# Adding the output projection's head-pair sums in DRAM in the first half of an attention kernel

## The chip, the cores and the metric

The kernel runs on one core of a Trainium2 chip. A core has five engines with a queue of their own each: TensorE (PE in the profile, its weight loads shown apart as PEld), VectorE (DVE), ScalarE (ACT), GpSimd (POOL) and SyncE (SP), which here only issues DMAs. Each engine works through its queue in order, and an instruction that waits for a semaphore holds up all that stands behind it on the same engine. Sixteen DMA engines move the data that any queue asks for. The metric is the device time of one execution in microseconds.

## The reference

With x of shape 2048 x 640, the reference computes a gated attention block in float32:

```python
xn = layernorm(x)
q  = (xn @ wq), as 32 heads of 128
p  = softmax(q @ k.T / sqrt(128))     # over the last 512 cached keys of each head
s  = concat_heads(p @ v) @ wo         # 4096 -> 640
g  = silu(relu(xn @ w1 + b1)**2 @ w2 + b2)
out = x + s * g
```

What matters here is the projection with `wo`: it sums over all 32 heads. The kernel takes the heads in pairs, so each 640 x 512 tile of `s` is a sum of 16 terms.

## The kernel before

The 2048 rows are cut into four tiles of 512. First the gate `g` is computed for three of the tiles; then comes the attention, in two halves (`hf`) of two tiles (`t`) each. Within a half the order is: for each of 16 head pairs (`g`), for each of the two tiles, for each of the two heads: one unit. There are 128 units, numbered `i`; an odd `i` ends a head pair for its tile. The gate of the fourth tile is worked into the start and the end of the attention.

Every product is made of three matmuls on a high and a low part of each operand. So a high part is made by ScalarE (a copy that rounds) and a low part by VectorE or GpSimd (a subtraction). One unit on the engines:

- TensorE: 12 matmuls for the scores `s` (`s_mm`, four banks), 15 for the query projection of a later unit (`q_mm`), 12 for the output `o` of the unit before (`v_mm`, four chunks of keys, the first two of which use the first half of the probabilities), and on average 15 for the projection with `wo` (`r_mm`; 30 for each head pair, in five blocks `d` of 128 output columns).
- VectorE: column maxima (`max_fold`), the shift `e = s - max` (`shift`), low parts of `q` and `o`, the sums of the softmax (`s_fold`), the normalisation (`o_norm`), and the additions of `r_acc`.
- ScalarE: `expo` (exponentials, two halves `k`), `p_hi` (high parts of the probabilities), `gather`, `q_hi`, `o_hi`, and the high parts of the weights (`prep`).
- GpSimd: `p_lo(i, 0)`, `s_add`, `p_lo(i, 1)` (low parts of the two halves of the probabilities, and the sum for the softmax), and the low parts of the weights (`prep`).
- SP: it writes the maxima to DRAM (`m_d`) and loads them back spread over all partitions (`bm`), the same for the softmax sums (`s_d` from `rows`, back as `bs`), and loads the raw weights behind `bs`.

The order of all this is written out by hand: `at(when, f, ...)` and `on(when, f, ...)` put a call into a plan with a nominal time, the plan is sorted by time, and the calls are issued in that order (`PERIOD` is the nominal unit). So each engine's queue holds its instructions in the order of the plan. The wrapper `Ordered` at lines 69 to 85 issues them, which is why nearly all of them carry line 77 in the profile and are told apart by the names of their tiles.

The projection's results come in two PSUM banks that are shared with the queries (`bank`, line 566). `r_acc` (line 753) empties them:

```python
        if g == 0:
            ...
            act.activation(ACC[hf, t][:, d, :], pr, AF.Copy)
        else:
            a = ACC[hf, t][:, d, :]
            dve.tensor_tensor(a, pr, a, op=ALU.add)
```

So for the first head pair ScalarE copies the bank to an accumulator in SBUF, and for the other 15 VectorE adds the bank to it. The tag `acc` has two buffers of 128 x 5 x 512, one for each tile of a half. The five `r_acc` of a head pair lie at about 3.0, 3.3, 4.0, 4.3 and 4.7 units after the start of its last unit in the order `d0`, `d1`, `d3`, `d2`, `d4` (line 1098; nominal times in `R_AT`, line 1038): `d0` and `d1` in an even unit, `d3`, `d2` and `d4` in an odd one. At the end of the first half `store_acc` (line 766) writes the accumulators to the DRAM tensor `s_d[t]`, and much later, one by one among the units of the second half, `load_finish`, `finish_gate` and `finish` read them back and make the output. In the second half the accumulator stays in SBUF to the end.

Of the kernel before, what the change touches and what calls it, by code (L numbers as in the profile page):

```python
# [8 lines left out]
F32 = mybir.dt.float32  # L9
F32R = mybir.dt.float32r  # L10
AF = mybir.ActivationFunctionType
ALU = mybir.AluOpType
AX = mybir.AxisListType

P = 128
NT = 512
# [9 lines left out]
def kernel(  # L26
# [20 lines left out]
    DC = D // P  # L47
# [21 lines left out]
    class Ordered:  # L69
# [13 lines left out]
    pe, dve, act, pool, sp = (  # L83
        Ordered(e) for e in (nc.tensor, nc.vector, nc.scalar, nc.gpsimd, nc.sync)
    )
# [5 lines left out]
    s_d = [dpool.tile([P, DC, NT], F32, name=f"s_d{t}") for t in range(NTILE // 2)]  # L91
# [15 lines left out]
    keep = ctx.enter_context(tc.tile_pool(name="keep", bufs=1))  # L107
# [375 lines left out]
    def mlp_step(n):  # L483
# [54 lines left out]
    TPH = NTILE // HALF  # L538
# [10 lines left out]
    PERIOD = 12.4  # L549
# [5 lines left out]
    XT, ACC, KT, VV, WQ, WO, Q, E, SC, MB, RD, PT, PO, OT, RB, QPS, FX, CL, PRS, RAW = (  # L555
        {} for _ in range(20)
    )
# [195 lines left out]
    def r_acc(i, d):  # L753
        hf, g, t, h = units[i]
        pr = PRS.pop((i, d))
        if g == 0:
            if d == 0:
                ACC[hf, t] = keep.tile(
                    [P, DC, NT], F32, tag="acc", name=f"acc{hf}_{t}", bufs=TPH
                )  # L760
            act.activation(ACC[hf, t][:, d, :], pr, AF.Copy)
        else:
            a = ACC[hf, t][:, d, :]
            dve.tensor_tensor(a, pr, a, op=ALU.add)

    def store_acc(t, d):
        sp.dma_start(s_d[t][:, d, :], ACC[0, t][:, d, :])

    def load_finish(n, hf, t, d):
        t0 = (hf * TPH + t) * NT  # L770
# [231 lines left out]
    def at(when, f, *a):  # L1002
        plan.append((max(when, 0.0), len(plan), f, a))

    for n in range(HALF * NG):
        hf, g = divmod(n, NG)
# [43 lines left out]
    for i in range(NU):  # L1050
        t0 = i * PERIOD

        def on(when, f, *a):
            at(t0 + when, f, *a)

        hf, g, t, h = units[i]
        for c in range(KC):
            on(0.68 * c, align, i, SLOTS[c])
            on(0.68 * c, s_mm, i, c)
        on(0.68 * KC - 0.6, align, i, SLOTS[KC])  # L1060
        qs = [(i + AHEAD, 3.45 if i % G and i > UPG else 4.3, 4.1)]
        if i == 0:
            qs = [(1, 2.8, 4.1), (2, 9.1, PERIOD - 5.2)]
        elif i < UPG:
            qs = [(i + 2, 4.9 if i == 3 else 4.2, 4.1)]
        for n, q_at, low in qs if i + AHEAD < NU else ():
            for c in range(DC):
                on(q_at + 0.68 * c, q_mm, n, (c,))
            on(q_at + 3.5, q_hi, n)
            on(q_at + low, q_lo, n)  # L1070
        for c in range(KC):
            on(0.8 + 0.68 * c, max_fold, i, c)
        on(3.95, gather, i, "m")
        on(4.1, row, i, "m")
        for c in range(KC):
            on(10.4 + 0.4 * c, shift, i, c)
        on(11.7, expo, i, 0)
        on(12.7, p_hi, i, 0)
        on(13.8, expo, i, 1)
        on(PERIOD + 4.0, p_hi, i, 1)  # L1080
        on(13.9, p_lo, i, 0)
        on(16.2, s_add, i)
        on(PERIOD + 6.2, s_fold, i)
        on(PERIOD + 8.0, gather, i, "s")
        on(PERIOD + 8.5, row, i, "s")
        on(18.6, p_lo, i, 1)
        for c in range(KC):
            on(PERIOD + 8.5 + 0.68 * c, v_mm, i, c)
        on(2 * PERIOD + 4.2, o_norm, i)
        on(2 * PERIOD + 4.9, o_hi, i)  # L1090
        on(2 * PERIOD + 5.5, o_lo, i)
        if i % G == G - 1:
            for d in range(DC):
                last = i == NU - G - 1
                if i < NU - 1:
                    for when, js in (R_AT_END if last else R_AT)[d]:
                        on(when, r_mm, i, d, js, (R_BANK_END if last else R_BANK)[d])
                    on(when + 0.68 * len(js), r_acc, i, d)
                if g == NG - 1 and hf == 0:
                    at((i + (3, 4, 5, 4, 5)[d] + (t and d in (0, 3, 4))) * PERIOD + 4.3, store_acc, t, d)  # L1100
                    w = (NU // 2 + 9 + 4 * (t * DC + d)) * PERIOD
                    for k, n in enumerate("sxg"):
                        at(w + k * PERIOD - 0.6, load_finish, n, 0, t, d)
                    at(w + 3 * PERIOD - 0.7, finish_gate, 0, t, d)
                    at(w + 3 * PERIOD - 0.7, finish, 0, t, d)
# [10 lines left out]
    for item in order:  # L1116
        kind, n = item[0], int(item[1:] or 0)
        if kind == "u":
            UP_AT[n] = now
        elif kind == "d":  # L1120
            DOWN_AT[n] = now
            at(now, late_down, n, range(DC))
        elif kind == "r":
            at(now, r_mm, NU - 1, n, range(G), (n + 1) % 2)
            at(now + 1.36, r_acc, NU - 1, n)
        else:
            for k, d in enumerate(range(DC)):
                for f in range(FA, FC):
                    DOWN_AT.setdefault(f, now)
                    at(now + 0.68 * ((FC - FA) * k + f - FA), late_down, f, (d,))  # L1130
                at(now + 0.68 * (FC - FA) * (k + 1), late_gate, d)
        now += STEP[kind]
# [110 lines left out]
```

## Time and profile before

| | |
|---|---|
| median of 3 runs | 1958.72 us (1958.57 to 1959.38) |
| profiled execution, span from first to last instruction | 1956.9 us |
| what lies around the span, against the median | 1.8 us |
| TensorE, weight loads | 1949.2, 1612.5 us busy |
| VectorE, ScalarE, GpSimd | 1537.3, 1187.6, 1376.7 us busy |
| granted TensorE clock | 1.000 |
| DMA on SP's queue (q1) and GpSimd's (q0) | 202.75 MB and 14.42 MB |

No time of its own is given for the profiled execution beside its span; the difference of 1.8 us to the median stands for what lies around. How to read the rows: a row of the timeline gives start, duration, engine, line, operation, the tile written and the tiles read, and in brackets the idle time before and what ended it. A group row gives busy time and mean nanoseconds of one instruction. A row of DMA issues gives the KB of each and the microseconds from issue to landing.

### The profile page before, as it was taken

The page shows a single profiled execution, that of the slowest core. Times are in us where ns is not written, and L with a number is a line of the kernel's source. Part 1 is how long each engine was busy: PE and PEld are TensorE (multiplying, and loading weights), DVE is VectorE, ACT ScalarE, POOL GpSimd, SP SyncE. Part 2 cuts the span into 40 slices and gives each one's busy share as a digit, 9 for nine tenths or more (in the row PEclk, how much of TensorE's full clock was granted, in tenths as well). Part 3 has the DMA queues.
Part 4 walks back from the last instruction along what each step waited for, and adds up shares of the span by engine and source line. Part 5 has one row for each costly group of instructions (what it writes and reads, how often), then busy time and mean ns, then how long its engine had stood idle before and what let it go on. Part 6 is the DMA issues. An engine that isn't in the chain of part 4 may idle for free.

```text
span 1956.9 us, 28182 instructions
## 1 busy us (share of the span) xinstructions
PE 1949.2 (100%) x8612; PEld 1612.5 (82%) x8612; DVE 1537.3 (79%) x2638; ACT 1187.6 (61%) x2040; POOL 1376.7 (70%) x757
## 2 busy tenths in 40 slices
PE   9999999999999999999999999999999999999998
PEld 7888888888888888888888888888888888888887
DVE  6523337788888888888888878888888888888865
ACT  5432336766666666666666676666666666666643
POOL 2121226888888888888888888888888888888841
PEclk9999999999999999999999999999999999999999
DMA  6330454333333332332335434433333333332353
GB/s 189 88 119 28 185 198 130 97 94 92 93 92 93 92 92 92 92 92 93 93 91 179 141 117 109 114 114 114 114 113 114 113 114 114 98 92 92 85 189 118
DMA packets 127892, 219.13 MB, mean 112 GB/s; under 512 B 23452, under 2 KB 38086, under 8 KB 126470
## 3 DMA queue, kind: packets, MB, share of 16 engines
q1 hardware_dynamic: 124742, 202.75, 34.3%
q0 software_dynamic: 2864, 14.42, 1.8%
q8 instruction: 77, 1.26, 0.2%
q14 instruction: 65, 0.53, 0.1%
q10 hardware_dynamic: 144, 0.16, 0.0%
HBM read 193.41 MB, written 23.87 MB: 111 GB/s over the span
## 4 chain that ended last, share of the span: by engine, by line
PE 99%; DVE 0%; DMA 0%; ACT 0%; issue 0%; POOL 0%; POOLq 0%
PE pq L77 22%; PE r L77 22%; PE o L77 18%; PE s L77 18%; PE ph L431 7%; PE ly L77 2%; PE py L101 2%; PE py L100 2%; PE py L102 2%; PE lu L77 2%; PE eu L77 1%; PE ph L398 0%; PE py L454 0%; PE py L453 0%; DMA xb<-in_x_dram 0%; PE px L77 0%
## 5 line engine op out<-in xcount | busy, mean ns | idle before, releaser
L77 POOL TENSOR_TENSOR pt<-e,pt 128x1024 fp32r<-128x1024 f32 x256 | 615.8, 2405 | 113.6 <-ACT pt L77 68.2
L77 PE MATMUL r<-ot,wo 128*128 128x512 f32 x1920 | 496.6, 389 | 0.0
L77 PE MATMUL pq<-ax,wq 128*128 128x512 f32 x1920 | 456.1, 389 | 0.0
L77 PEld LDWEIGHTS pq<-ax,wq 128*128 128x128 f32 x1920 | 360.4, 188 | 75.2 <-DVE q L77 0.4
L77 PEld LDWEIGHTS r<-ot,wo 128*128 128x128 f32 x1920 | 360.5, 188 | 74.8
L77 PE MATMUL o<-pt,wv 128*128 128x512 f32 x1536 | 369.2, 389 | 0.0
L77 PE MATMUL s<-q,wk 128*128 128x512 f32 x1536 | 369.0, 389 | 0.0
L77 DVE TRANSPOSE_TENSOR_REDUCE rdm<-s 128x16 f32<-128x512 f32 x512 | 347.6, 712 | 6.0 <-PE s L77 5.8
L77 ACT ACTIVATE e<-e 128x1024 f32<-128x1024 f32 x256 | 269.8, 1054 | 123.8 <-DVE e L77 80.5
L77 PEld LDWEIGHTS o<-pt,wv 128*128 128x128 f32 x1536 | 288.3, 188 | 60.1 <-POOL pt L77 0.4
L77 PEld LDWEIGHTS s<-q,wk 128*128 128x128 f32 x1536 | 288.4, 188 | 59.8
L77 DVE TENSOR_TENSOR e<-s,bm 128x512 f32<-128x512 f32 x512 | 312.3, 665 | 5.8 <-DMA bm<-m_d 5.4
L77 POOL TENSOR_TENSOR su<-e,e 128x1024 f32<-128x1024 f32 x128 | 309.2, 2415 | 0.0
L77 ACT ACTIVATE pt<-e 128x1024 fp32r<-128x1024 f32 x256 | 271.9, 1062 | 6.9
L77 DVE TENSOR_TENSOR acc<-r,acc 128x512 f32<-128x512 f32 x300 | 203.6, 679 | 12.7 <-PE r L77 12.4
L77 ACT ACTIVATE rdm<-rdm 32x64 f32<-32x64 f32 x384 | 97.7, 254 | 182.1 <-DVE rdm L77 179.0
L77 DVE TRANSPOSE_TENSOR_REDUCE rds<-su 128x32 f32<-128x1024 f32 x128 | 158.4, 1237 | 0.3 <-POOL su L77 0.3
L77 DVE TENSOR_TENSOR ot<-o,ot 128x512 fp32r<-128x512 f32 x128 | 88.5, 692 | 86.1 <-ACT ot L77 86.1
L77 ACT ACTIVATE q<-pq 128x512 fp32r<-128x512 f32 x128 | 76.7, 599 | 113.6 <-PE pq L77 113.6
L431 PE MATMUL ph<-xT,w1s 128*128 128x512 f32 x585 | 139.0, 389 | 0.0
L431 PEld LDWEIGHTS ph<-xT,w1s 128*128 128x128 f32 x585 | 109.7, 188 | 22.8
L77 ACT ACTIVATE rds<-rds 32x32 f32<-32x32 f32 x384 | 89.7, 234 | 60.1 <-DVE rds L77 56.6
(137 smaller groups left out, 1942.3 us busy)
## 6 DMA issues: line engine op xcount, KB each, us to landing
bm<-m_d SPq DMA_DIRECT2D x128, 256.0 KB, 3.2
bs<-s_d SPq DMA_DIRECT2D x128, 256.0 KB, 4.0
qr<-in_wq_dram SPq DMA_DIRECT2D x64, 320.0 KB, 4.5
or<-in_wo_dram SPq DMA_DIRECT2D x64, 320.0 KB, 4.7
kr<-in_kT_dram SPq DMA_DIRECT2D x64, 256.0 KB, 4.3
vr<-in_v_dram SPq DMA_DIRECT2D x64, 256.0 KB, 4.3
xT_d<-xT POOLq DMA_DIRECT2D x6, 1280.0 KB, 7.6
ax<-xT_d SPq DMA_DIRECT2D x4, 1280.0 KB, 11.3
```

The costliest lines, as they stand in the source:

```text
L77: ins = method(*args, **kwargs)
L100: nc.tensor.matmul(ps, ah, bh, start=first and i == 0, stop=False)
L101: nc.tensor.matmul(ps, ah, bl, start=False, stop=False)
L102: nc.tensor.matmul(ps, al, bh, start=False, stop=last and i == n - 1)
L431: nc.tensor.matmul(ph, w1s[f][i][:, c, :], xs[j][:, c, :], start=k == 0, stop=k == len(order) - 1,)
```

## The change

In the first half (`hf == 0`) `r_acc` lets ScalarE copy every bank, for all 16 head pairs, to a tile of the tag `acc`, which is now taken anew for each head pair. After the copy of the last block (`d == DC - 1`) GpSimd's queue issues one DMA of the whole tile (1280 KB) to `s_d[t]`: a plain write for the first head pair, and for the other 15 a DMA that adds to what is there, in descriptors of at most 5120 bytes, so two for each of the 128 partitions. The ten stores `store_acc` on SP's queue and their places in the plan are gone. The second half is as before.

```diff
     def r_acc(i, d):
         hf, g, t, h = units[i]
         pr = PRS.pop((i, d))
-        if g == 0:
+        if hf == 0:
+            if d == 0:
+                ACC[hf, t] = keep.tile(
+                    [P, DC, NT], F32, tag="acc", name=f"part{i}", bufs=TPH
+                )
+            act.activation(ACC[hf, t][:, d, :], pr, AF.Copy)
+            if d == DC - 1:
+                how = {} if g == 0 else {"accum_op": ALU.add, "max_dma_last_dim": 2 * DC * NT}
+                pool.dma_start(s_d[t], ACC[hf, t], **how)
+        elif g == 0:
             if d == 0:
                 ACC[hf, t] = keep.tile(
                     [P, DC, NT], F32, tag="acc", name=f"acc{hf}_{t}", bufs=TPH
...
         else:
             a = ACC[hf, t][:, d, :]
             dve.tensor_tensor(a, pr, a, op=ALU.add)
-
-    def store_acc(t, d):
-        sp.dma_start(s_d[t][:, d, :], ACC[0, t][:, d, :])
...
                 if g == NG - 1 and hf == 0:
-                    at((i + (3, 4, 5, 4, 5)[d] + (t and d in (0, 3, 4))) * PERIOD + 4.3, store_acc, t, d)
                     w = (NU // 2 + 9 + 4 * (t * DC + d)) * PERIOD
```

## The prediction

> **What bounds the kernel now.** Begin with the page's head, busy shares and chain of waits.
>
> ```profile
> span 1956.9 us, 28182 instructions
> PE 1949.2 (100%) x8612; PEld 1612.5 (82%) x8612; DVE 1537.3 (79%) x2638; ACT 1187.6 (61%) x2040; POOL 1376.7 (70%) x757
> PE 99%; DVE 0%; DMA 0%; ACT 0%; issue 0%; POOL 0%; POOLq 0%
> ```
>
> The chain is TensorE from end to end. Next, the timeline of TensorE gives the start of the score matmuls of two units far apart, and of two neighbours:
>
> ```profile
> 383.03 1.29 PE L77 MATMUL s<-q,wk 128*128 128x512 f32 x5
> 603.35 2.88 PE L77 MATMUL s<-q,wk 128*128 128x512 f32 x12
> 615.59 2.88 PE L77 MATMUL s<-q,wk 128*128 128x512 f32 x12
> 1851.83 1.52 PE L77 MATMUL s<-q,wk 128*128 128x512 f32 x6
> ```
>
> 615.59 - 603.35 = 12.24 us, and (1851.83 - 383.03) / 12.24 = 120.0 units: one pace, in both halves and while the first half's sums are handed over. A unit is 54 matmuls (12 scores, 12 outputs, 15 queries, 15 projection), so 226.7 ns each. No unit is shorter than another, so TensorE waits for nobody here, and freeing VectorE can't shorten a unit. What the change can do to the time is add a wait.
>
> The wait nearest to happening is the one for GpSimd's low part of the probabilities, `p_lo(i, 1)`. It happened once, in the start-up:
>
> ```profile
> 341.22 2.40 POOL L77 TENSOR_TENSOR pt<-e,pt 128x1024 fp32r<-128x1024 f32 x1
> 343.68 0.99 PEld L77 LDWEIGHTS o<-pt,wv 128*128 128x128 f32 x5 [0.37 <-POOL pt L77]
> ```
>
> GpSimd ended at 343.62 and the eighth weight load of `o` started 0.06 us later: that load needs `p_lo(i, 1)`.
>
> **Part 1: 150 sums leave VectorE, 150 copies come to ScalarE.** By groups of instructions:
>
> ```profile
> L77 DVE TENSOR_TENSOR acc<-r,acc 128x512 f32<-128x512 f32 x300 | 203.6, 679 | 12.7 <-PE r L77 12.4
> L77 ACT ACTIVATE acc<-r 128x512 f32<-128x512 f32 x20 | 11.8, 588 | 3.8 <-PE r L77 3.6
> ```
>
> VectorE loses 150 x 0.679 = 101.9 us (half of the 300, the first half's), ScalarE gains 150 x 0.588 = 88.2 us. Neither sets the pace, so the gain is nothing; the question is what stands behind each copy on ScalarE's queue. The trace already holds the answer: the first head pair of the second half is copied by ScalarE in the same places, at full pace. Its timeline, with an even unit starting at 1154.15 (615.59 + 44 x 12.24):
>
> ```profile
> 1148.51 2.43 POOL L77 TENSOR_TENSOR pt<-e,pt 128x1024 fp32r<-128x1024 f32 x1
> 1149.85 2.68 PEld L77 LDWEIGHTS o<-pt,wv 128*128 128x128 f32 x12
> 1151.91 0.58 ACT L77 ACTIVATE acc<-r 128x512 f32<-128x512 f32 x1
> 1152.08 1.57 POOL L77 TENSOR_TENSOR wq<-qr,wq 128x640 fp32r<-128x640 f32 x1 [1.14 <-ACT wq L77]
> 1152.25 2.48 DVE L77 TENSOR_TENSOR e<-s,bm 128x512 f32<-128x512 f32 x4 [0.20 <-DMA bm<-m_d]
> 1156.26 2.41 POOL L77 TENSOR_TENSOR pt<-e,pt 128x1024 fp32r<-128x1024 f32 x1 [1.35 <-issue]
> 1160.99 2.41 POOL L77 TENSOR_TENSOR pt<-e,pt 128x1024 fp32r<-128x1024 f32 x1
> 1162.09 2.68 PEld L77 LDWEIGHTS o<-pt,wv 128*128 128x128 f32 x12
> 1164.05 2.43 DVE L77 TENSOR_TENSOR e<-s,bm 128x512 f32<-128x512 f32 x4
> 1166.59 0.60 ACT L77 ACTIVATE acc<-r 128x512 f32<-128x512 f32 x1 [0.15 <-PE r L77]
> ```
>
> Read off the margins. The eighth weight load is due 7 x 0.2267 = 1.59 us after the first. Odd unit: 1149.85 + 1.59 - 0.06 - (1148.51 + 2.43) = 0.44 us. Even unit: 1162.09 + 1.59 - 0.06 - (1160.99 + 2.41) = 0.22 us. In the odd unit ScalarE also has 0.15 us in which the copy of `d3` waits for its matmul, so the even unit's shift (1164.05, the input of that chain) may come 0.15 + 0.44 = 0.59 us later before TensorE waits. Copies alone: cost 0, between 0 and nothing below, since this pair ran at 12.24. Their cover is these 0.2 to 0.6 us, where the same waits had more room before:
>
> ```profile
> 621.50 2.42 POOL L77 TENSOR_TENSOR pt<-e,pt 128x1024 fp32r<-128x1024 f32 x1
> 623.53 2.68 PEld L77 LDWEIGHTS o<-pt,wv 128*128 128x128 f32 x12
> ```
>
> 623.53 + 1.59 - 0.06 - 623.92 = 1.14 us. If the cover goes, each late microsecond is paid once per pair of units.
>
> **Part 2: the DMA on GpSimd's queue.** 32 DMAs are issued (16 head pairs, 2 tiles), 30 of them accumulating. Each waits on GpSimd for the copy of `d4`; behind it stand low parts of weights and then `p_lo(i, 0)`. What a plain one costs there:
>
> ```profile
> L77 POOL DMA_DIRECT2D xT_d<-xT x16 | 8.9, 556 | 0.0
> xT_d<-xT POOLq DMA_DIRECT2D x6, 1280.0 KB, 7.6
> bm<-m_d SPq DMA_DIRECT2D x128, 256.0 KB, 3.2
> bs<-s_d SPq DMA_DIRECT2D x128, 256.0 KB, 4.0
> s_d<-acc SPq DMA_DIRECT2D x10, 256.0 KB, 3.9
> ```
>
> For tile 0 the copy of `d4` ends at 1152.49 and the low part of `wq` at 1153.65, and the issue goes between that and `wv`; before `p_lo(i, 0)` GpSimd idles 1.35 us, which hides 0.56. For tile 1 the issue stands one odd unit later, where GpSimd waits for ScalarE's `wo`; more room. An accumulating issue has 256 rows of 5 KB where a plain one has 128, and two reads a row: 0.56 to 4 x 0.56 = 2.2 us. I take about 1 us, nearer the row, and hidden: 0. At 2.2 it would cost 2.2 - 1.35 - 0.22 = 0.6 us for each of tile 0's 15.
>
> SP loses the ten stores of the last row; nothing waits for SP's issue there: 0. Their successor, the last accumulating DMA, is issued near 1127, and the reload of the sums starts at 1191.5 (rows below), so nothing waits there either.
>
> ```profile
> L77 SPq DMA_DIRECT2D s_d<-acc x10: 425/430/435, 1088.4 to 1149.1; - x10
> L77 SPq DMA_DIRECT2D fs<-s_d x10: 375/376/433, 1191.5 to 1632.4; - x10
> ```
>
> A tile's buffer is written again by the `d0` copy of its next pair. For tile 0 the `d4` copy above ends at 1152.49; the `d0` copy of tile 1 is at 1154.60, tile 0's next one two units later, about 1179.1: 26.6 us, and a DMA that lands within that delays no copy.
>
> ```profile
> 1154.60 0.58 ACT L77 ACTIVATE acc<-r 128x512 f32<-128x512 f32 x1
> 1175.62 0.57 ACT L77 ACTIVATE acc<-r 128x512 f32<-128x512 f32 x1
> ```
>
> The second row is tile 1's `d4` copy, two units less 0.77 us after that of tile 0 (1151.91).
>
> **Part 3: what the DMA does to the loads beside it.** This is the disputed term. Two views of the DMA queues, each one microsecond long: GpSimd's queue alone (213 to 214), and beside loads from SP (210 to 211); columns are packets, MB, share of 16 engines.
>
> ```profile
> q0 software_dynamic: 54, 0.43, 101.7%
> ...
> q1 hardware_dynamic: 97, 0.22, 55.6%
> q0 software_dynamic: 33, 0.22, 51.7%
> ```
>
> A plain 1.31 MB takes 1.31 / 0.43 = 3.05 us of all engines. Adding in DRAM moves the bytes up to three times (read both, write one): 3.05 to 9.15 us. No run shows it; with the second read on the same engines at least partly in turn I take 2.5 passes, 7.6 us, one row of 5 KB on an engine 7.6 / 16 = 0.48 us. The loads that share the time (`bs` and two weights, 0.85 MB) add 0.85 / 0.43 = 2.0 us, so the DMA is in flight 9.6 us. Issued at 613.2 (tile 1: 1176.19 less 46 units) or 615.1 (tile 0: 1153.65 less 44 units) in the time of the unit of 603.35, with about 1.1 us to the first byte, it ends near 623.9 or 625.8. These loads lie in it:
>
> ```profile
> 614.63 0.32 SPq L77 DMA_DIRECT2D bs<-s_d  x1
> 620.52 0.33 SPq L77 DMA_DIRECT2D m_d<-rowm  x1
> 621.02 0.68 DVE L77 TENSOR_TENSOR o<-o,bs 128x512 f32<-128x512 f32 x1
> 621.89 0.33 SPq L77 DMA_DIRECT2D bm<-m_d  x1
> ```
>
> `bs` lands at 618.6 and is used at 621.0: 2.4 us of room. `bm` lands at 625.09; the shift that needs it would start at 615.59 + (1164.05 - 1154.15) = 625.49: 0.40 of room, and 0.59 from part 1: 0.99 us. In the shared microsecond three packets of SP went by for one of GpSimd's (97 to 33). `bm` has 8 packets of 2 KB on each engine, so it lets 8/3 = 2.7 rows past: 2.7 x 0.48 = 1.28 us; `m_d` waits for one, 0.48. Late: 1.76 - 0.99 = 0.77 us for tile 0. For tile 1 only about half of `bm` is caught: 0.64 + 0.48 - 0.99 = 0.13. `bs` loses 1.28 of its 2.4.
>
> **Sum.** 15 x 0.77 + 15 x 0.13 = 13.5 us, all on TensorE's path; parts 1 and 2 nothing. Against the profiled span 1956.9 + 13.5 = 1970.4; the median of the runs, 1958.72, lies 1.8 us above that span, so 1972. Ends of the unknown: one pass (ends by 621.3, before `bm` moves) gives 0; three passes (0.57 us a row, both tiles caught in full: 1.52 + 0.57 - 0.99 = 1.10 x 30) gives 33 us, 1992.
>
> **Rivals.**
> *Hidden anyway.* The DMA is through before 621 or the loads slip past, and the time is 1958.7 to 1960. For it: the pair copied by ScalarE ran at 12.24; in the shared microsecond SP's queue still moved 0.22 MB, hardly less than `bm` needs. It decides at two passes: then tile 1's DMA ends at 622.4, before `bm` moves. That VectorE's 102 us bring nothing belongs to this case too.
> *The DMA far slower, or its packets taken in turn one for one.* `bm` then lets 8 rows past: 8 x 0.48 + 0.48 - 0.99 = 3.3 us, in 30 places 100 us: 2058. Against it: the 97 to 33 above; for it: those were loads with a full queue. With rows of 1 us at three for one it is 2.7 + 1 - 0.99 = 2.7, 80 us: 2040; above 26.6 us in flight the copies of ScalarE would wait as well.
> [...]
> *GpSimd's issue becomes the bound.* At 2.2 us each, 15 x 0.6 and for tile 1 about half as much: 13 us, 1972, with SP's loads on time.
>
> **How the numbers follow.** Within 0.2% (3.9 us) is about what a measurement can tell from no change. Chances: `bm` late, 1963 to 1998, 0.40; hidden, 0.31; far slower 0.10 and one for one 0.07, 1998 to 2060; GpSimd's issue, 0.07; another wait that I don't see, 0.02; faster, 0.03, since only start-up waits such as the 0.37 us above could go. Slower: 0.66; same: 0.31; faster: 0.03. The forecast is the first case, 1972, its own range 1963 to 1998; the range for 8 in 10 takes in the hidden case and part of the slow one: 1957 to 2025.
>
> **What the profile after would show.** Right: `acc<-r` 150 on VectorE and 170 on ScalarE; 32 issues on GpSimd's queue; q0 up by 42 MB or more; score starts of the first half more than 12.24 us apart, second half unchanged; VectorE's shift of even units idle before it, released by `bm`; weight loads of `o` idle, released by GpSimd's `pt`; landing of `bm` up in the first half's even units. Wrong: first half at 12.24 (hidden); issues of 2 us on GpSimd with `bm` on time (the third rival); landing over 20 us, with ScalarE's copies waiting for a DMA (the second).

## The result and the profile after

The changed kernel takes 2086.46 us, median of 4 runs (2085.6 to 2089.6), where the kernel before took 1959.05 in 4 runs on the same chip (1958.57 to 1959.92). The ratio is 1.0653, with an interval of 1.0641 to 1.0666. The change costs 127 us, 4.2 us for each of its 30 adding DMAs. That the time rises, because small loads come late and TensorE waits, was forecast. The size was not: 1972 was said, and the range ended at 2025. Nor were the places where TensorE waits.

The page of the changed kernel, in the order in which that of before was read: the span, the busy shares, the chain of waits by engine, and GpSimd's DMA queue (packets, MB, share of 16 engines).

```profile
span 2087.8 us, 28249 instructions
PE 2001.3 (96%) x8612; PEld 1636.1 (78%) x8612; DVE 1450.2 (69%) x2488; ACT 1253.8 (60%) x2190; POOL 1410.5 (68%) x789
q0 software_dynamic: 11312, 56.36, 12.1%
PE 68%; DMA 16%; DVE 7%; ACT 4%; issue 2%; POOL 2%; SPq 0%; POOLq 0%; ACTq 0%
```

The span grew by 2087.8 - 1956.9 = 130.9 us. VectorE lost its 150 sums (1537.3 to 1450.2 us busy), and that brought nothing. The chain, TensorE from end to end before, now goes through a DMA for 16% of the span. Where the time went is in the groups of TensorE's matmuls, and in the group of VectorE's shift (busy us, mean ns, idle before and what ended it):

```profile
L77 PE MATMUL r<-ot,wo 128*128 128x512 f32 x1920 | 510.4, 397 | 38.1 <-DVE q L77 38.1
L77 PE MATMUL s<-q,wk 128*128 128x512 f32 x1536 | 399.1, 412 | 37.2 <-DVE e L77 37.1
...
L77 PE MATMUL o<-pt,wv 128*128 128x512 f32 x1536 | 371.6, 390 | 3.4 <-POOL pt L77 3.4
...
L77 DVE TENSOR_TENSOR e<-s,bm 128x512 f32<-128x512 f32 x512 | 313.2, 668 | 66.8 <-DMA bm<-m_d 65.8
```

TensorE waits 38.1 + 37.2 + 3.4 = 78.7 us in the attention, where its list of waits had none of these before, and it is busy 2001.3 - 1949.2 = 52.1 us longer with the same 8612 matmuls. Together that is 130.8 of the 130.9 us. The list of waits (total us, times, longest) says what is behind both:

```profile
DVE o L77 <- DMA bs<-s_d: 76.9, 17, 5.7
DVE e L77 <- DMA bm<-m_d: 65.8, 18, 6.2
PE r L77 <- DVE q L77: 38.1, 15, 3.4
PE s L77 <- DVE e L77: 37.1, 16, 5.3
```

So there are two places, about one visit for each head pair and tile. Some 16 times the scores wait for VectorE's shift `e`, which waits for the maxima (`m_d`, then `bm`). Some 15 times the projection waits for VectorE's `q`, which stands on its queue behind the normalisation of `o`, which waits for the softmax sums (`bs`).

The first place, a DMA of tile 0, in the timeline of the changed kernel (start, duration, engine, operation, in brackets the idle time before):

```profile
707.39 1.19 POOL L77 DMA_DIRECT2D s_d<-part  x1
...
712.99 0.33 SPq L77 DMA_DIRECT2D m_d<-rowm  x1
...
718.83 0.33 SPq L77 DMA_DIRECT2D bm<-m_d  x1
...
722.17 2.48 DVE L77 TENSOR_TENSOR e<-s,bm 128x512 f32<-128x512 f32 x4 [4.14 <-DMA bm<-m_d]
722.91 4.61 PE L77 MATMUL s<-q,wk 128*128 128x512 f32 x12 [2.45 <-DVE e L77]
```

`bm` reads what `m_d` wrote, and its issue is SP's wait for it: 718.83 - 712.99 = 5.84 us, where the kernel before took 621.89 - 620.52 = 1.37. VectorE then idles 4.14 us and TensorE 2.45. And the twelve scores take 4.61 us instead of 2.88. The second place, a DMA of tile 1:

```profile
734.76 1.20 POOL L77 DMA_DIRECT2D s_d<-part  x1 [1.47 <-ACT part L77]
...
736.18 0.32 SPq L77 DMA_DIRECT2D bs<-s_d  x1
...
746.66 0.70 DVE L77 TENSOR_TENSOR o<-o,bs 128x512 f32<-128x512 f32 x1 [4.87 <-DMA bs<-s_d]
...
750.50 2.58 PE L77 MATMUL r<-ot,wo 128*128 128x512 f32 x6 [2.56 <-DVE q L77]
```

Here `bs` is in flight from 736.18 to about 746.6, 10.4 us, where it took 4.0 before. The DMA queues in windows of the changed kernel (714 to 716, then 743 to 744; packets, MB, share of the engines) show SP's packets beside the adding ones:

```profile
q0 software_dynamic: 80, 0.41, 101.6%
...
q0 software_dynamic: 32, 0.16, 81.4%
q1 hardware_dynamic: 30, 0.06, 18.3%
```

In the first window, one and three microseconds after `m_d` was issued, SP's queue moves no packet at all. Its 80 adding rows took all engines for 2 us, so one row takes 2 x 16 / 80 = 0.40 us. Later, at 743, the two queues go one for one, 32 packets to 30 (a packet in these rows is one row). So the share was none to 80 in one window and 30 to 32 in the other, and neither is the 97 to 33 on which the forecast rested. How many rows go by ahead of `m_d` is measured below, and it is no fixed number.

The slow scores are the granted clock. The view by windows of the changed kernel (the number after the five engines' busy times is the clock):

```profile
719.00:722.90 3.90, 1.46 (x7) 0.89 (x5) 0.73 (x2) 0.00 (x0) 1.76 (x2) 1.00 0.28 73
722.91:727.52 4.61, 4.61 (x13) 3.69 (x14) 3.80 (x6) 3.43 (x4) 1.35 (x1) 0.63 0.51 187
727.52:730.00 2.48, 2.48 (x12) 2.03 (x12) 1.03 (x2) 1.68 (x5) 2.48 (x2) 1.00 0.01 3
```

0.63 over 4.61 us is (1 - 0.63) x 4.61 / 0.5 = 3.4 us at half clock, behind the wait of 2.45 us, and full clock again after it. The trace's clock records hold 23 such stretches, 85.3 us in all, and every one follows a wait of TensorE of 1.8 us or more. But not every such wait has one: of the 29 waits of that length in the attention 6 have none. Two waits of the same 2.56 us show the difference (they end at 864.23 and at 1034.13):

```profile
860.15:863.56 3.41, 1.52 (x7) 0.94 (x5) 2.51 (x4) 1.08 (x2) 0.00 (x0) 1.00 0.13 46
863.56:866.97 3.41, 2.57 (x10) 1.83 (x11) 2.99 (x8) 2.23 (x6) 1.89 (x2) 1.00 0.14 47
1030.82:1034.23 3.41, 0.85 (x5) 0.39 (x3) 2.59 (x4) 1.76 (x5) 0.00 (x0) 1.00 0.19 63
1034.23:1037.64 3.41, 3.41 (x8) 2.68 (x9) 3.20 (x7) 2.39 (x5) 2.66 (x2) 0.50 0.09 32
```

All 23 stretches begin a whole number of times 3.413 us apart and last 3.413 us, two of them twice that, so the attention of this trace can be counted in slots of that length. In 21 slots TensorE idled 1.95 us or more, and every one is followed by a slot at half clock. Of the five with 1.79 to 1.90 us three are. Of those with 1.7 us or less one is, with 1.05 us, and it was itself at half clock. The wait at 1034.13 lies in one slot; the one at 864.23 is split into 1.89 and 0.67 us. The mean clock is 0.979 where it was 1.000: up to 0.021 x 2087.8 = 44 of the 52 us by which TensorE was busy longer (85.3 us at half clock lose 42.7).

The second half is as before; two neighbouring units still stand 12.24 us apart:

```profile
1847.92 2.88 PE L77 MATMUL s<-q,wk 128*128 128x512 f32 x12
...
1860.16 2.88 PE L77 MATMUL s<-q,wk 128*128 128x512 f32 x12
```

### The profile page after: what moved, and what is told of

Same layout as the page of the kernel before. It is cut to its first block, busy times and chain, and to the rows that moved or that the text cites. A ratio compares the mean times of both kernels' runs of the same rounds, so it can differ in the third digit from the quotient of the medians.

```text
span 2087.8 us, 28249 instructions
## 1 busy us (share of the span) xinstructions
PE 2001.3 (96%) x8612; PEld 1636.1 (78%) x8612; DVE 1450.2 (69%) x2488; ACT 1253.8 (60%) x2190; POOL 1410.5 (68%) x789
## 4 chain that ended last, share of the span: by engine, by line
PE 68%; DMA 16%; DVE 7%; ACT 4%; issue 2%; POOL 2%; SPq 0%; POOLq 0%; ACTq 0%
PE r L77 15%; PE s L77 13%; PE pq L77 12%; PE o L77 10%; DMA bs<-s_d 6%; PE ph L431 6%; DMA m_d<-rowm 5%; DMA bm<-m_d 3%; DVE rdm L77 2%; PE ly L77 2%; PE py L101 2%; PE py L100 2%; PE py L102 2%; PE lu L77 2%; DVE rds L77 2%
## 5 line engine op out<-in xcount | busy, mean ns | idle before, releaser
L77 PE MATMUL r<-ot,wo 128*128 128x512 f32 x1920 | 510.4, 397 | 38.1 <-DVE q L77 38.1
L77 PEld LDWEIGHTS r<-ot,wo 128*128 128x128 f32 x1920 | 366.1, 191 | 121.5 <-DVE q L77 44.8
L77 PE MATMUL s<-q,wk 128*128 128x512 f32 x1536 | 399.1, 412 | 37.2 <-DVE e L77 37.1
L77 PEld LDWEIGHTS s<-q,wk 128*128 128x128 f32 x1536 | 306.8, 201 | 113.1 <-DVE e L77 46.4
L77 DVE TENSOR_TENSOR e<-s,bm 128x512 f32<-128x512 f32 x512 | 313.2, 668 | 66.8 <-DMA bm<-m_d 65.8
L77 POOL TENSOR_TENSOR wv<-vr,wv 128x512 fp32r<-128x512 f32 x64 | 90.0, 1406 | 108.8 <-ACT wv L77 101.7
L77 DVE TENSOR_TENSOR o<-o,bs 128x512 f32<-128x512 f32 x128 | 87.0, 679 | 76.9 <-DMA bs<-s_d 76.9
L77 ACT ACTIVATE ot<-o 128x512 fp32r<-128x512 f32 x128 | 76.5, 597 | 89.7 <-DVE o L77 89.7
## 6 DMA issues: line engine op xcount, KB each, us to landing
s_d<-part POOLq DMA_DIRECT2D x32, 1280.0 KB, 12.3
```

The costliest lines, as they stand in the source:

```text
L77: ins = method(*args, **kwargs)
```

## The experiments

Each edit is against the changed kernel, unless it says otherwise. Letters in the expectations stand for theories as told there; the text after each says in words what fell or stood. "Cost" is the median less that of the kernel before on the same chip.

**The copies alone.** The accumulators are copied as in the change, but only the last head pair is written.

```diff
-            if d == DC - 1:
-                how = {} if g == 0 else {"accum_op": ALU.add, "max_dma_last_dim": 2 * DC * NT}
-                pool.dma_start(s_d[t], ACC[hf, t], **how)
+            if d == DC - 1 and g == NG - 1:
+                pool.dma_start(s_d[t], ACC[hf, t])
```

> ScalarE copies all 160 banks of the first half as in the changed kernel, but GpSimd issues only two DMAs, plain ones after the last head pair (so the sums of the 15 other head pairs are left out of the first half). Theory A (the adding DMA holds the DMA engines, SP's small loads come late): no cost without the DMAs, 1957 to 1962 us. Rival B (the copies and the new order on ScalarE cost the time): near 2086.

Measured: 1961.37 us (10 runs) against 1958.67, ratio 1.0013 (1.0003 to 1.0022). The page's head:

```profile
span 1960.0 us, 28160 instructions
PE 1950.7 (100%) x8612; PEld 1611.5 (82%) x8612; DVE 1450.5 (74%) x2488; ACT 1256.5 (64%) x2190; POOL 1375.8 (70%) x759
```

TensorE is busy the whole span although ScalarE has all 150 copies. The time is the one of theory A, and rival B has fallen. The copies cost 2.7 us; the rest, some 125 us, comes with the DMAs.

**The same bytes without the adding.** The 30 DMAs write and don't add.

```diff
-                how = {} if g == 0 else {"accum_op": ALU.add, "max_dma_last_dim": 2 * DC * NT}
+                how = {} if g == 0 else {"max_dma_last_dim": 2 * DC * NT}
```

> As the changed kernel, all 32 DMAs with the same rows of 5120 bytes, but each writes plainly and adds nothing (the sums over head pairs are left out of the first half). Theory A (a row that is read, added and written takes 0.40 us of an engine, and about eight of them go through before SP's queue gets its turn): a plain row takes 0.19 us, eight of them 1.5 us; the write of the maxima is late by about 1.5 us where 0.99 is free: 0.5 x 15 = 8 us or less, 1959 to 1975. Rival C (any 1.28 MB on GpSimd's queue does it): near 2086. Rival D (the issue of 256 rows, 1.2 us on GpSimd, is what costs): near 2086 too, with the issue still at 1.2 us.

Measured: 2005.83 us (4 runs), ratio 1.0241 (1.0226 to 1.0256), a cost of 47 us. Its groups and its landing time:

```profile
L77 PE MATMUL o<-pt,wv 128*128 128x512 f32 x1536 | 377.5, 391 | 10.3 <-POOL pt L77 10.2
...
L77 PE MATMUL s<-q,wk 128*128 128x512 f32 x1536 | 372.5, 391 | 18.5 <-DVE e L77 18.3
...
s_d<-part POOLq DMA_DIRECT2D x32, 1280.0 KB, 7.9
```

So a plain store of 1280 KB in these places already delays the maxima (VectorE's shift waits 59.4 us for `bm`, where it was 5.4 in the kernel before) and makes TensorE wait 10.3 + 18.5 = 28.8 us, and the time is above the 1959 to 1975 that the theory of the adding alone gave, and well below the 2086 of rival C. Rival D's condition was not met: a plain issue of these rows took 0.73 us. The wait at the projection is gone: VectorE waits for `bs` 16.1 us in all, where it was 76.9. The longest of TensorE's waits here is 1.6 us and the mean clock is 0.999. In a microsecond in which it has the engines to itself (964 to 965) the plain DMA shows:

```profile
q0 software_dynamic: 83, 0.42, 102.1%
```

That is 16 / 83 = 0.193 us for a row of 5 KB; a row that adds, at 0.40, takes 2.1 times as long. The other 80 us of the change come with the adding, and more than half of them may be the clock (42.7 us are lost at half clock in the change).

**Five DMAs for each head pair.** Each block is sent on its own, as soon as it is copied.

```diff
-            if d == DC - 1:
-                how = {} if g == 0 else {"accum_op": ALU.add, "max_dma_last_dim": 2 * DC * NT}
-                pool.dma_start(s_d[t], ACC[hf, t], **how)
+            how = {} if g == 0 else {"accum_op": ALU.add}
+            pool.dma_start(s_d[t][:, d, :], ACC[hf, t][:, d, :], **how)
```

> The adding DMA is cut into five of 256 KB, each issued right behind its copy, in rows of 2 KB. Theory A: eight rows of about 0.16 us on an engine, 1.3 us in one go; SP's small DMAs are late by at most that, 0.3 us past the margin: 1960 to 1980. Rival D (GpSimd's issues): five of 0.6 to 1.2 us in a head pair, 3 to 6 us where GpSimd idles 4.6: 1975 to 2060, with weight loads of o released by GpSimd's pt.

Measured: 2058.72 us, ratio 1.0511 (1.0495 to 1.0527), clock 0.999.

```profile
L77 PE MATMUL o<-pt,wv 128*128 128x512 f32 x1536 | 388.6, 395 | 59.6 <-POOL pt L77 59.6
...
L77 PE MATMUL s<-q,wk 128*128 128x512 f32 x1536 | 372.0, 391 | 13.4 <-DVE e L77 13.4
...
L77 POOL DMA_DIRECT2D s_d<-part x160 | 162.8, 1017 | 96.2 <-DVE rdm L77 85.0 <-ACT part L77 11.0
```

The waits for the maxima fall from 37.2 to 13.4 us, since each DMA lands in 4.5 us and not in 12.3. But now GpSimd spends 162.8 us on issues, and TensorE waits 59.6 us for its low parts. The time lies in the 1975 to 2060 of rival D, above theory A's 1960 to 1980. This is how the rival "GpSimd's issue becomes the bound" looks; in the change itself that row is 3.4 us.

**Is it one long packet of GpSimd's queue?** Two edits of the same line, the first asking for a single packet, the second halving the rows.

```diff
-                how = {} if g == 0 else {"accum_op": ALU.add, "max_dma_last_dim": 2 * DC * NT}
+                how = {} if g == 0 else {"accum_op": ALU.add, "max_dma_last_dim": 2 * DC * NT, "single_packet": True}
```

> As the changed kernel, but the rows of an engine are marked as a single packet. Theory A1 (the eight rows that go through in one go are a packet of the software queue): now all 16 rows, 6.4 us, go in one go; the write of the maxima and the loads of the softmax sums come some 3 us later still: 30 x 2 to 3 us more, 2145 to 2190. Theory A2 (the burst is set by something else, such as rows already fetched ahead): same as the changed kernel, 2080 to 2095.

```diff
-                how = {} if g == 0 else {"accum_op": ALU.add, "max_dma_last_dim": 2 * DC * NT}
+                how = {} if g == 0 else {"accum_op": ALU.add, "max_dma_last_dim": DC * NT}
```

> As the changed kernel, the adding DMA in rows of 2560 bytes (512 rows, 32 on an engine) where it had 5120. Rows of 2 KB took 0.177 us and of 5 KB 0.402 us, so 0.215 us each and 6.9 us of an engine in all, as against 6.4. Theory A (a fixed number of rows goes through before SP's queue gets its turn): the waits of SP's small DMAs fall to about half, 2030 to 2060. Theory F (the write of the maxima stands behind the two weight loads on SP's own ring, and these share the engines with the whole of the DMA): no better than the changed kernel, 2080 to 2110, some of it from an issue of about 2 us on GpSimd.

Measured: 2089.44 us (ratio 1.0666, 1.0645 to 1.0688) and 2083.76 us (1.0638, 1.0617 to 1.0659), 2 runs each, against 2086.46. The single packet changes nothing, as theory A2 said, so the burst is not a matter of that setting. Nor does the time fall with the smaller rows, as it would by a fixed number of rows; it is in theory F's range, whose reason the next experiment tests. With rows of 2.5 KB (0.215 us each in the packet records) the waits only move: 92.4 us of VectorE's wait for `bm` instead of 65.8, 52.6 for `bs` instead of 76.9.

**Is it `m_d`'s place in SP's queue?** The maxima of the first half go out on ScalarE's queue, which has nothing else in flight.

```diff
-        sp.dma_start(d, r)
+        (act if what == "m" and units[i][0] == 0 else sp).dma_start(d, r)
```

> As the changed kernel, but in the first half the 2 KB write of the maxima is issued from ScalarE's queue, so it stands behind nothing of SP's. Theory F: beside an adding DMA it lands after 1.5 to 3.5 us instead of 5.3 to 6.5, and the total falls to 2030 to 2065 (ScalarE waits some 0.7 us in each unit, which takes a part back). Theory A: it still waits for the rows in front on the engine, lands after 5 us or more, and the total stays at 2080 to 2110.

Measured: 2085.77 us (2078.98 to 2090.83), ratio 1.0647 (1.0619 to 1.0674). A tile 0 case in its timeline:

```profile
648.41 1.19 POOL L77 DMA_DIRECT2D s_d<-part  x1
...
653.97 0.31 ACTq L77 DMA_DIRECT2D m_d<-rowm  x1
...
659.80 0.33 SPq L77 DMA_DIRECT2D bm<-m_d  x1
```

Alone on its queue `m_d` still takes 5.83 us. The DMA queues from 655 to 657.3, while it waits:

```profile
q0 software_dynamic: 96, 0.49, 105.9%
```

Only adding rows move. In the packet records the first packet of `m_d` starts 3.5 us after the start of its issue, where 0.8 is usual: it waits in the DMA engines for 2.7 us, some seven adding rows of 0.40. Then its 48 packets start over 2.0 us, among the adding rows, where 0.2 is usual; 2.7 + 1.8 us is all that it loses. (The expectation of the run with rows of 2.5 KB has 3.3 and 0.6; the difference is the same.) That the place in SP's queue makes the delay is refuted.

The same with plain stores, and with rows of 2.5 KB:

```diff
-        sp.dma_start(d, r)
+        (act if what == "m" and units[i][0] == 0 else sp).dma_start(d, r)
...
-                how = {} if g == 0 else {"accum_op": ALU.add, "max_dma_last_dim": 2 * DC * NT}
+                how = {} if g == 0 else {"max_dma_last_dim": 2 * DC * NT}
```

> The kernel with plain writes in place of the adding DMAs, and the write of the maxima on ScalarE's own ring in the first half. With plain writes on SP's ring the write of the maxima landed after 2.5 to 5.2 us, its packets right behind the last packet of the weight loads. Theory F (what is left of the cost with plain writes is that place in SP's ring): it lands after 1.3 to 2.5 us, seven plain rows of 0.196 us at most, and the total falls from 2006 to 1960 to 1985. If the engines hold it up in any case: 2000 to 2012.

```diff
-        sp.dma_start(d, r)
+        (act if what == "m" and units[i][0] == 0 else sp).dma_start(d, r)
...
-                how = {} if g == 0 else {"accum_op": ALU.add, "max_dma_last_dim": 2 * DC * NT}
+                how = {} if g == 0 else {"accum_op": ALU.add, "max_dma_last_dim": DC * NT}
```

> Adding DMAs in rows of 2560 bytes, and the write of the maxima on ScalarE's own ring. With rows of 5120 bytes on that ring its first packet came 3.3 us after the issue instead of 0.6: 2.7 us, seven rows of 0.402. Theory A2a (an engine has a fixed number of about seven rows taken up ahead): 7 x 0.215 = 1.5 us, landing after 3.3 to 4.0 us. Theory A2b (it has a fixed time or number of bytes taken up ahead): 2.7 us again, landing after 5 us or more. Total 2040 to 2085 in the first case, near 2084 in the second.

Measured: 2005.32 us with plain stores (ratio 1.0237, 1.022 to 1.0254), the same as with `m_d` on SP's queue, and beside tile 0's DMA `m_d` still takes 3.8 to 5.0 us; theory F has fallen here too. With adding rows of 2.5 KB it is 2055.45 us (1.049, 1.0469 to 1.0511), and the first packet of `m_d` again starts at 3.5 us, as theory A2b said, though the time is in the range of A2a. So the wait is not a fixed number of rows: 2.7 / 0.40 = 6.8 rows of 5 KB, 2.7 / 0.215 = 12.6 rows of 2.5 KB, about 32 to 34 KB for each engine in both. What holds that amount ahead is not shown. Nor is it settled why the time fell by 28 us with small rows and the own queue together; the clock (0.991 to 0.998) explains up to 0.007 x 2081 = 15 of them.

**Which tile's DMA makes which wait.** Only tile 0 sends its sums every head pair; tile 1's are written at the end.

```diff
-            if d == DC - 1:
-                how = {} if g == 0 else {"accum_op": ALU.add, "max_dma_last_dim": 2 * DC * NT}
+            if d == DC - 1 and (t == 0 or g == NG - 1):
+                how = {} if g == 0 or t else {"accum_op": ALU.add, "max_dma_last_dim": 2 * DC * NT}
```

> As the changed kernel, but only tile 0 gets its adding DMAs; tile 1 is only written once at the end of the half (the sums of 15 head pairs are left out for it). If each DMA costs by itself: about half of the 127 us, 2015 to 2030. Tile 0's DMA is issued together with the loads of the softmax sums and meets the write of the maxima: what is left should be TensorE's waits at the scores, released by VectorE's shift, and the waits at r, released by VectorE's low part of q, should be gone with tile 1's.

Measured: 2017.85 us, ratio 1.0301 (1.0281 to 1.0322), a cost of 59 us, near half.

```profile
L77 PE MATMUL r<-ot,wo 128*128 128x512 f32 x1920 | 497.6, 390 | 0.0
...
L77 PE MATMUL s<-q,wk 128*128 128x512 f32 x1536 | 381.6, 398 | 35.9 <-DVE e L77 35.8
```

This is as expected. The wait at the projection is gone, that at the scores has stayed (35.9 of 37.2). Tile 0's DMA meets `m_d`, tile 1's meets `bs`, and each pays for itself, about 4 us.

**Does a wait alone lower the clock?** The kernel before, with no DMA added: in odd units of the first half GpSimd does the second low part three times, which makes TensorE wait for it.

```diff
-        pool.tensor_tensor(PT[i, k][1], E[i, k], raw(PT[i, k][0]), op=ALU.subtract)
+        for _ in range(3 if k and i % G and units[i][0] == 0 else 1):
+            pool.tensor_tensor(PT[i, k][1], E[i, k], raw(PT[i, k][0]), op=ALU.subtract)
```

> The kernel before, without the change, but in the first half GpSimd makes the low part of the second half of the probabilities three times over for each odd unit (2 x 2.36 us more, the same result), so TensorE waits there once per head pair without any DMA. Margin 1.14 us or less: 3.5 to 4 us of wait in each of 32 places, 112 to 128 us. Theory G (a wait of about 2 us or more halves TensorE's clock for 3.4 us, whatever caused it): 1.7 us more in each place, granted clock of the run below 0.99, 2110 to 2145. Rival (the low clock comes of the DMAs or does not cost): clock 1.000 and 2070 to 2090.

Measured: 2150.65 us (2 runs), ratio 1.0979 (1.0943 to 1.1015). The groups, the list of waits and the clock:

```profile
PE 2036.7 (95%) x8612; PEld 1667.5 (77%) x8612; DVE 1540.9 (72%) x2638; ACT 1187.0 (55%) x2040; POOL 1523.3 (71%) x821
...
L77 PE MATMUL o<-pt,wv 128*128 128x512 f32 x1536 | 409.6, 415 | 111.2 <-POOL pt L77 111.2
```

```profile
PE o L77 <- POOL pt L77: 111.2, 32, 4.1
```

```profile
core 0: 2155.0 us, clock 0.952
```

The 32 waits are 3.5 us each and make 111.2 of the 198.1 us by which the span grew. The same matmuls were busy 2036.7 - 1949.2 = 87.5 us longer. There are 31 stretches at half clock, 204.8 us in all, 6.6 us each where 3.4 was expected; so the time is above the 2110 to 2145 of theory G, and far above its rival's. Here the waits alone, with no DMA added, lowered the mean clock to 0.952. And with the DMAs but shorter waits it stays at 0.999, in the plain stores above and in the last experiment.

**The DMA issued at another time.** The issue moves from behind the copy of `d4` to a later place in the plan.

```diff
-            if d == DC - 1:
-                how = {} if g == 0 else {"accum_op": ALU.add, "max_dma_last_dim": 2 * DC * NT}
-                pool.dma_start(s_d[t], ACC[hf, t], **how)
+    def add_part(i):
+        hf, g, t, h = units[i]
+        how = {} if g == 0 else {"accum_op": ALU.add, "max_dma_last_dim": 2 * DC * NT}
+        pool.dma_start(s_d[t], ACC[hf, t], **how)
...
+                if hf == 0:
+                    on(5 * PERIOD + 6.25, add_part, i)
```

> The changed kernel with its adding DMAs issued about 7 us later, on GpSimd behind the low part of the second half of the probabilities in the following even unit, so that they begin when the maxima have been loaded, and meet the writes and loads of the softmax sums (2.9 us of room) in place of the maxima (0.99 us). If the cost lies in which load is met: the waits at the scores go, 1965 to 2010. If any place costs as much: 2070 to 2100. It can't be under 1958, since the kernel before has TensorE at work all the time.

Measured: 3199.56 us, ratio 1.6328 (1.6304 to 1.6353). The edit stands in the loop over the five blocks, so each DMA was issued five times, 160 in all, and GpSimd waited for its own earlier DMA. It says nothing on the place. With each issued once:

```diff
-                if hf == 0:
+                if d == DC - 1 and hf == 0:
                     on(5 * PERIOD + 6.25, add_part, i)
```

> The changed kernel with each of the 32 DMAs issued once, as before, but about 7 us later: on GpSimd behind the low part of the second half of the probabilities of the following even unit. It then begins when the maxima have been loaded, and meets the writes and loads of the softmax sums (2.9 us of room) in place of the maxima (0.99 us). If the cost lies in which load is met: 1965 to 2010. If any place costs as much: 2070 to 2100.

Measured: 2027.18 us (4 runs), ratio 1.0346 (1.0329 to 1.0364), a cost of 68 us instead of 127; the 1965 to 2010 expected was missed.

```profile
L77 PE MATMUL r<-ot,wo 128*128 128x512 f32 x1920 | 501.8, 392 | 27.5 <-DVE q L77 27.5
...
L77 PE MATMUL o<-pt,wv 128*128 128x512 f32 x1536 | 378.3, 392 | 10.9 <-POOL pt L77 10.9
...
L77 PE MATMUL s<-q,wk 128*128 128x512 f32 x1536 | 374.5, 393 | 2.0 <-DVE e L77 1.7
```

The waits at the scores are gone. Now all DMAs meet `bs` (VectorE waits for it 31 times, 2.6 us on average), and TensorE waits about 0.9 us each time, nearly always too short for the clock, which is 0.999. In its 12.3 us of landing, or 10.6 here, the DMA covered one of the small loads in both places tried, and TensorE had no time to give. None of the versions came below the kernel before.

## Why the prediction was right in direction and wrong in size

- *TensorE is the bound and VectorE's 102 us bring nothing.* Right: with the copies alone the span is 1960.0 us and TensorE is busy for all but 0.5% of it.
- *Part 1, copies at no cost.* Right within what can be told: 2.7 us.
- *Part 2, an issue of about 1 us on GpSimd, hidden.* Right. The view of the tile `part` gives the median, 1203 ns, and TensorE's wait for GpSimd's low parts is 3.4 us in the whole execution.

```profile
L77 POOL DMA_DIRECT2D s_d<-part x32: 557/1203/1245, 370.4 to 1253.9; - x32
```

- *Part 3, the time of the DMA itself.* Nearly right: 2.1 plain passes where 2.5 were taken, 0.40 us a row where 0.48 was, 16 x 0.40 = 6.4 us of engines where 7.6 was. The 2.5 passes were an estimate that no run had shown, and what an adding DMA reads and writes for a row the runs don't show either, only its time. From issue to landing it is 12.3 us, where the forecast put about 1.1 to the first byte and 9.6 in flight.
- *Part 3, what the loads beside it lose.* This is the step that failed, in two sentences of it: "three packets of SP went by for one of GpSimd's" and "`m_d` waits for one, 0.48". `m_d`, 2 KB in all, lost 5.84 - 1.37 = 4.5 us, not 0.48: some seven rows went ahead of its first packet, and more among the others. The three-to-one share came from one microsecond in which SP's loads already flowed; it doesn't tell how long a new small DMA waits before its first packet. With that, 15 x 0.77 for tile 0 became 16 waits of 2.3 us.
- *The place of the wait.* This failed as well. The prediction let TensorE wait at the weight loads of `o`, for GpSimd's low part, behind 0.99 us of room. In the change TensorE waits 3.4 us there in all (7.4 in the row of the weight loads). For tile 0 it waits 37.1 us at the scores, for VectorE's shift, a wait that the prediction does not name: in the case shown VectorE idles 4.14 us and TensorE 2.45, so the room there is 1.7 us. The place named does show where the clock stays up: with plain stores the weight loads of `o` wait 22.5 us for `pt`.
- *Tile 1.* "`bs` loses 1.28 of its 2.4" was the same error: it was in flight 10.4 us instead of 4.0, lost 6.4 and came 4 us and more too late. So tile 1 cost as much as tile 0, where 0.13 us was said, by a wait that the sum did not contain.
- *The clock.* Not in the sum at all. Waits were priced at their own length, and 23 of the long ones brought at least 3.4 us at half clock behind them. In the case shown the wait is 2.45 us and the slow scores take 1.73 more, 4.2 us. The mean of the 30 DMAs is the same: 78.7 / 30 = 2.6 us of waits and 52.1 / 30 = 1.7 of longer matmuls, of which the clock explains 42.7 / 30 = 1.4. Not shown is what the time would be at full clock; a part of the slow time may stand in for waits at `o` that would follow.
- *The rivals.* "Hidden anyway" fell. "Far slower, or one for one" came nearest in time (2040 to 2058), and the one for one did occur, at 743. But its price was put on `bm`, with one row for `m_d`, and the far slower DMA did not occur. "GpSimd's issue" fell for the change, and showed itself only with five issues a head pair. Of the signs named for the right case two failed: the weight loads of `o` wait little for `pt`, and the landing of `bm` did not go up (3.1 us, where it was 3.2), because what is late is its issue.

```profile
s_d<-part POOLq DMA_DIRECT2D x32, 1280.0 KB, 12.3
bm<-m_d SPq DMA_DIRECT2D x128, 256.0 KB, 3.1
```

## What to carry to other kernels

Where the bounding engine never waits, ask of every new large transfer which small round trip it will meet and how long that trip's first packet may stand behind it; a share of bandwidth measured between two flowing queues didn't answer that here (97 to 33 packets, and 2.7 us of standing behind). Price the wait that results with the clock behind it: here 2.6 us of waiting cost 4.2 on average. Follow the late tile to every engine that reads it, and to the first wait that this makes on the bounding engine. A transfer that is in flight for most of a period was moved here but not hidden, and it cost least where the wait it makes stayed short (68 us instead of 127).

## What was not expected of the hardware

- A small DMA on a queue of its own started 2.7 us late behind an adding DMA of GpSimd, and about the same with rows of 5 KB and of 2.5 KB. Behind the plain rows of tile 0's DMA its first packet started 1.4 to 1.6 us after the issue instead of 0.8, and its last 3.1 to 4.2 instead of 1.0. Why is open.
- Adding in DRAM took 0.40 us for a 5 KB row on one engine, a plain write 0.193.
- In the changed kernel waits of TensorE of 1.8 to 2.6 us could be followed by 3.4 us at half clock, where about 1.9 us of idle time or more fell in one slot of 3.413 us. Where all or nearly all waits stayed at or under 1.7 us (plain stores, five DMAs, the later place) the mean clock was 0.999. Behind the waits of 3.5 us, with no DMA added, the low stretches were 204.8 / 31 = 6.6 us long.
- With the clock at 0.999, TensorE's busy time still rose, by 2002.2 - 1956.9 - 28.8 = 16.5 us with the plain stores. Half of it is in the group of `o` (369.2 to 377.5 us), whose weight loads wait 22.5 us for `pt` where its matmuls show 10.2. The rest the rows don't tell.
